# Reciprocal of the softmax sums before the transpose instead of behind it, and another place for the routing constants, in a fused attention and mixture kernel

## The chip, the cores and the metric

One Trainium2 chip, one of its cores. The metric is the device time of one execution in microseconds (us). The engines are named as in the profile: PE (matrix products; PEld is its weight loading), DVE (vector), ACT (scalar), POOL (GpSimd) and SP (here only issues transfers).

## The reference, cut to what matters

Attention over 4 batches of 8 heads, 576 positions of 64 elements, causal and with a decay bias; its output goes through a three-way max layer and then through a routed layer with one of 8 experts for each of the 2304 tokens.

```python
def _attn_ref(q, k, v, s):
    scores = scale * np.matmul(q, k.transpose(0, 1, 3, 2))
    ...
    bias = -(cum[:, :, :, None] - cum[:, :, None, :])
    scores = np.where(causal, -1000000000.0, scores + np.minimum(bias, 0.0))
    attn = np.exp(scores - np.max(scores, axis=-1, keepdims=True))
    attn = attn / (np.sum(attn, axis=-1, keepdims=True) + 1e-09)
    return np.matmul(attn, v)

def _moe_ref(x, w1, w2, w3, w_out):
    h = np.maximum(np.maximum(x @ w1, x @ w2), x @ w3)
    return h @ w_out

def _moe2_ref(x, modality_id, w_gate, modality_bias, w1, w2):
    logits = x @ w_gate + modality_bias[modality_id]
    e_idx = np.argmax(logits, axis=1)
    ...
    for e in range(E):
        h = np.maximum(x[e_idx == e] @ w1[e], 0.0)
        out[e_idx == e] = gate_w[e_idx == e, None] * (h @ w2[e])
```

The change touches the division by the sums (with the 1e-09 added to them) and the time at which constants of the routing are prepared: the table of token numbers, the bias of the modality, an upper triangle for counting.

## The kernel before, in words

The work has three stages: attention (up to about 250 us), the three-way max layer with its output product and the routing (to about 550 us), and the experts (to the end). Products in near float32 precision are made of three passes over a rounded high part and a low part, which ACT rounds and DVE or POOL subtracts.

Attention goes through 16 couples of heads (`for p in range(1, NP)` with couple 0 ahead of it); a couple shares the 128 partitions for its values. For each head `front` loads the head that is three ahead (L_AHEAD), splits the next one (`split`, S_AHEAD) and calls `scores`. There the 576 rows fall into five chunks of 128 rows (QC), and six banks of scores are made: two matmuls each into a tile `s_ps` of a pool of three banks (lines 248 and 249), one DVE reduction that scales, masks and takes the row minimum `mn` (line 250), and an exponential on ACT for each chunk that also sums into `l` (line 252). The scaled scores stand in one of four buffers `e`. Every couple has one tile `l` of 128 rows by 2 heads x 5 chunks.

A couple's remaining work is put off: `turn()`, which calls `inverse` for couple p - 1, runs after the first head of couple p, and `drain` then turns the two heads (`turned`: 15 transposes a head through four tiles `t_ps` of a pool of three banks, each copied into a `pt` by ACT or DVE in turn) and multiplies them with the values (`values_of`: twelve matmuls in a fixed order, then two DVE multiplications with `rb`, lines 301 and 302). `inverse` transposes `l` to 10 rows of 128 (line 261) into a tile of that same pool `t_ps`, adds 1e-9 on ACT on the way out of it (line 263), takes the reciprocal on DVE (line 264), stores the result to DRAM and loads it back spread over 64 partitions for each head as `rb` (lines 265 and 268).

When the four couples of a batch are done, first-layer products for it (`fill`, lines 149 to 153, with the `h` maxima of line 325) are put between the heads that follow, by a list `todo` of due times. Weights are converted early in couples 1 to 8 (`convert`, `converted`).

`tables()` (lines 372 to 401) prepares the constants: seven transfers on SP, five instructions on POOL and seven on DVE, none on ACT or PE. It is called in couple 12 (`P_SET`), inside `tc.issue_after(exps[-1])`.

A scheduler sets the order on every engine: it goes through the program with estimated times and places what is ready; `tc.issue_after(x)` keeps the marked instructions behind `x` where both are on one engine. So the order in the program is not the order on the engines, and each engine then executes its own in order and waits for the others by semaphores.

Of the kernel before, what the change touches and what calls it, by code (L numbers as in the profile page):

```python
# [5 lines left out]
F32 = mybir.dt.float32  # L6
# [3 lines left out]
ALU = mybir.AluOpType  # L10
ACTF = mybir.ActivationFunctionType
# [75 lines left out]
def fused_kernel(tc, qk, vd, sd, w64, mod, wg, wgt, mb, we, cst, csi, out):  # L87
    nc = tc.nc
    V, A, G, P, SP = nc.vector, nc.scalar, nc.gpsimd, nc.tensor, nc.sync
    top = ExitStack()  # L90
    with top:
# [13 lines left out]
        ident = per.tile([128, 128], F32, name="ident")  # L105
# [5 lines left out]
        bias = per.tile([128, NT, E], F32, name="bias")  # L111
# [45 lines left out]
        with ExitStack() as es:  # L157
# [17 lines left out]
            ss = es.enter_context(tc.tile_pool(name="ss", bufs=4))  # L175
# [5 lines left out]
            mask = ap1.tile([128, S], F32, name="mask")  # L181
# [11 lines left out]
            last_load = [None]  # L193


            def load(p, j):
                x = qkp.tile([128, 2, S], F32, name="qk_r", bufs=QR_BUFS)
                k_b = qkp.tile([66, S], F32R, name="k_b", bufs=KB_BUFS)
                for t in (range(2) if p == 0 else ()):
                    (SP, A)[t if j == 0 else 0].dma_start(out=x[:, 1 - t], in_=qk[PORD[p], :, 1 - t, j])  # L200
                if p == 0:
                    A.dma_start(out=k_b.bitcast(F32)[64:66], in_=augk.bitcast(F32)[16 * j + PORD[0]:16 * j + PORD[0] + 1])
                    if j == 0:
                        SP.dma_start(out=mask[:, S - 128:S], in_=cst[:, 256:384])
                        SP.dma_start(out=ident, in_=cst[:, 0:128])
                else:
                    SP.dma_start(out=x, in_=qk[PORD[p], :, :, j])
                    last_load[0] = SP.dma_start(out=k_b.bitcast(F32)[64:66], in_=dk[PORD[p], :, j]).ins
                return p, j, x, k_b


            def split(t):
                p, j, x, k_b = t
                hl = qkp.tile([128, 2, S], F32R, name="hl", bufs=HL_BUFS)
                q_b = qbs[(2 * p + j) % len(qbs)]
                A.copy(out=hl[64:128, 0], in_=x[64:128, 1])
                A.copy(out=hl[:, 1], in_=x[:, 0])
                G.tensor_copy(out=k_b[0:64], in_=x[0:64, 1])
                V.tensor_tensor(out=hl[0:64, 0], in0=x[64:128, 1], in1=hl.bitcast(F32)[64:128, 0], op=ALU.subtract)  # L219
                ins = G.tensor_tensor(out=q_b[0:64], in0=x[0:64, 0], in1=hl.bitcast(F32)[0:64, 1], op=ALU.subtract).ins  # L220
                return ins, (hl, q_b, k_b)

            def values_in(p):
                v_r = vp.tile([128, 5, 128], F32, name="v_r")
                SP.dma_start(out=v_r, in_=vd[PORD[p]])
                return v_r

            def scores(j, qkb):
                hl, q_b, k_b = qkb
                e = e_bufs[n_e[0] % E_N]  # L230
                n_e[0] += 1
                mn = ss.tile([128, 5], F32, name="mn")
                if j == 0:
                    sums.append(ss.tile([128, 2, 5], F32, name="l"))
                l = sums[-1][:, j]
                banks = [None] * len(SPACK)
                for c, (q0, _, w) in enumerate(QC):

                    nq = 128
                    ec = e[:, EOFF[c]:EOFF[c] + w]  # L240
                    m0 = 448 if c == 0 else S - w
                    first = 3.0e38
                    for k0, n in [(0, w)] if c < 4 else [(0, 288), (288, 288)]:
                        bi, o = next((i, o) for i, bank in enumerate(SPACK) for cc, kk, o in bank if (cc, kk) == (c, k0))
                        if banks[bi] is None:
                            banks[bi] = ps_s.tile([128, 512], F32, name="s_ps")
                        s_ps = banks[bi][0:nq, o:o + n]
                        P.matmul(s_ps, hl[:, 1, q0:q0 + nq], hl[:, 0, k0:k0 + n], start=True, stop=False)  # L248
                        ins = P.matmul(s_ps, q_b[:, q0:q0 + nq], k_b[:, k0:k0 + n], start=False, stop=True).ins  # L249
                        V.tensor_tensor_reduce(out=ec[:, k0:k0 + n], in0=s_ps, in1=mask[0:nq, m0 + k0:m0 + k0 + n], scale=-0.125, scalar=first, op0=ALU.add, op1=ALU.min, accum_out=mn[0:nq, c:c + 1])  # L250
                        first = mn[0:nq, c:c + 1]
                    ex = A.activation(out=ec, in_=ec, func=ACTF.Exp, bias=mn[0:nq, c:c + 1], scale=-1.0, accum_out=l[0:nq, c:c + 1]).ins  # L252
                    if c >= 2:
                        gates.append(ins)
                exps.append(ex)
                return e


            def inverse(p, l):
                r_ps = ps_t.tile([128, 512], F32, name="t_ps")[0:10, 0:128]  # L260
                P.transpose(out=r_ps, in_=l.rearrange("p j c -> p (j c)"), identity=ident)
                r_t = ss.tile([10, 128], F32, name="r_t")
                A.activation(out=r_t, in_=r_ps, func=ACTF.Copy, bias=1e-9)
                V.reciprocal(out=r_t, in_=r_t)
                SP.dma_start(out=r_d[p], in_=r_t)
                rb = vp.tile([128, 640], F32, name="rb")
                for j in range(2):
                    SP.dma_start(out=rb[j * 64:(j + 1) * 64], in_=r_d[p:p + 1, 5 * j:5 * j + 5].rearrange("a c n -> a (c n)").to_broadcast([64, 640]))
                return rb
# [59 lines left out]
            parts = {0: load(0, 0)}  # L329
# [10 lines left out]
            def front(h):  # L340
                n = h + L_AHEAD
                if n < 2 * NP:
                    parts[n] = load(*divmod(n, 2))
                n = h + S_AHEAD
                if n < 2 * NP:
                    parts[n] = split(parts[n])[1]
                return scores(h % 2, parts.pop(h))

            behind = []
# [1 line left out]
            exps = []  # L351
            sums = []
            last_t = [None]

            def drain(keep):
                while len(behind) > keep:
                    p, es_, v_r, rbs, pts = behind.pop(0)
                    pts.append(turned(es_[len(pts)], len(pts)))
                    if len(pts) == 2:
                        values_of(p, v_r, rbs[0], pts)  # L360
# [45 lines left out]
            for p in range(1, NP):  # L406
                v_r = values_in(p)
                es_ = []
                for j in range(2):
                    es_.append(front(2 * p + j))  # L410
                    if j == 0:
                        turn()
                    drain(1 - j)
                    if j == 1:
                        turn = queue(p, es_, v_r)
                    n_head += 1
                    while todo and todo[0][0] < n_head:
                        at, job = todo.pop(0)
                        with tc.issue_after(gates[int(at * 3)]):
                            job()  # L420
                if p == NP - 1:
                    turn()
                    drain(0)
                with tc.issue_after(exps[-1 - CONV_LAG]), tc.issue_after(last_load[0]):
                    for w in raws:
                        converted(*w)
                    raws = [convert(n // 3, n % 3, w0p, "w0", rawp, early=True) for n in CONV.get(p, ())]
                if p == P_SET:
                    with tc.issue_after(exps[-1]):
                        tables()  # L430
                if p % (H // 2) == H // 2 - 1:
                    b = PORD[p] // (H // 2)
                    n = 0
                    for i in range(b * S // FW, (b + 1) * S // FW if NFILL[b] else 0):
                        xx, hs = [], {}
                        todo.append((n_head + FILL_0 + n * FILL_N[b] / (6 * NFILL[b]), lambda i=i, xx=xx: xx.extend(fill_x(i, fxp, "fx", V if XL_V else G))))
                        for f in range(NFILL[b]):
                            for j in range(3):
                                todo.append((n_head + FILL_0 + n * FILL_N[b] / (6 * NFILL[b]), lambda i=i, f=f, j=j, xx=xx, hs=hs: fill(i, f, j, xx, hs, ps_f, fhp, "fh")))
                                n += 1  # L440
# [467 lines left out]
```

## Time and profile before

| what | value |
|---|---|
| median of 3 runs | 752.18 us (748.55 to 752.93) |
| the profiled execution | 752.2 us |
| its span, first to last instruction | 750.3 us |
| PE busy | 719.6 us (96%) |
| DVE busy | 529.4 us (71%) |
| ACT busy | 404.4 us (54%) |
| POOL busy | 181.6 us (24%) |

The busy times are of the whole span, and the stages differ: an engine with a low share can still set the pace of one of them. A matmul's end is modelled, so a PE that counts as busy need not go at its full rate. Idle time of an engine is put down to the event that ended it.

### The profile page before, as it was taken

To read this page: it belongs to the slowest core of one execution; us is meant where nothing else is said; L and a number is where in the kernel's file an instruction comes from. 1 tells how busy PE (TensorE), PEld (TensorE's weight loads), DVE (VectorE), ACT (ScalarE), POOL (GpSimd) and SP (SyncE) were. 2 spreads that over 40 slices of the span, in tenths; PEclk is the share of its full clock that TensorE was granted. 3 is DMA by queue.
4 is the path that set the end of the run, shared out by engine and by line. 5 is a ranking of instruction groups with operands and counts; after the bars stand their busy time and mean duration, and the time that the engine had idled before them with its cause. 6 is when DMAs were issued, how large, how long until landed. Compare 5 with 4: busy or idle time off the path is not lost. (4 is left out here: it accounts for less than half of the span.)

```text
span 750.3 us, 13624 instructions
## 1 busy us (share of the span) xinstructions
PE 719.6 (96%) x4602; PEld 642.7 (86%) x4602; DVE 529.4 (71%) x1567; ACT 404.4 (54%) x976; POOL 181.6 (24%) x202
## 2 busy tenths in 40 slices
PE   3898999899999999999999999999999999999996
PEld 3665798788998899899999898989899988999884
DVE  6899979987776589692958796737677556575540
ACT  6887878876775445222222322536546556565631
POOL 6346554544340100010010101032222222222101
PEclk9999999999999999999999999999899999999999
DMA  8476665674321174101101101847547675756610
GB/s 234 132 233 206 211 200 171 192 240 141 113 71 46 41 271 153 37 14 22 43 22 53 50 21 51 282 146 219 182 156 234 213 252 181 244 212 208 230 40 18
DMA packets 45104, 108.56 MB, mean 145 GB/s; under 512 B 8992, under 2 KB 12992, under 8 KB 45024
## 3 DMA queue, kind: packets, MB, share of 16 engines
q1 hardware_dynamic: 37368, 90.75, 37.3%
q0 software_dynamic: 4912, 11.82, 5.0%
q10 hardware_dynamic: 2744, 5.02, 1.9%
q8 instruction: 38, 0.62, 0.4%
q14 instruction: 42, 0.34, 0.1%
HBM read 93.55 MB, written 12.18 MB: 141 GB/s over the span
## 5 line engine op out<-in xcount | busy, mean ns | idle before, releaser
L149 PE MATMUL a_ps<-xh,w_h 128*128 128x384 f32 (+2 forms) x492 | 159.0, 324 | 0.2
L152 PE MATMUL a_ps<-xl,w_h 128*128 128x384 f32 (+2 forms) x492 | 158.2, 322 | 0.0
L153 PE MATMUL a_ps<-xh,w_l 128*128 128x384 f32 (+2 forms) x492 | 157.1, 320 | 0.0
L608 DVE TENSOR_TENSOR e_l<-e_raw,e_h 128x512 fp32r<-128x512 f32 x160 | 103.3, 687 | 15.6 <-ACT e_h L607 9.8
L607 ACT CAST e_h<-e_raw 128x512 fp32r<-128x512 f32 x160 | 93.1, 623 | 21.5 <-DMA e_raw<-in_we 7.6
L252 ACT ACTIVATE e<-e,mn 128x64 f32<-128x64 f32 (+4 forms) x160 | 89.2, 559 | 17.7 <-DVE mn L250 17.4
L149 PEld LDWEIGHTS a_ps<-xh,w_h 128*128 128x128 f32 x492 | 92.6, 188 | 1.6 <-DVE h L325 0.6
L152 PEld LDWEIGHTS a_ps<-xl,w_h 128*128 128x128 f32 x492 | 92.6, 188 | 0.4
L153 PEld LDWEIGHTS a_ps<-xh,w_l 128*128 128x128 f32 x492 | 92.6, 188 | 0.2
L248 PE MATMUL s_ps<-hl 128*128 128x64 f32 (+2 forms) x192 | 66.3, 356 | 16.4 <-DVE hl L219 9.2
L641 PE MATMUL h_ps<-x2t,e_h 128*128 128x256 f32 x288 | 81.8, 285 | 0.0
L642 PE MATMUL h_ps<-x2t,e_l 128*128 128x256 f32 x288 | 81.5, 284 | 0.0
L638 PE MATMUL h_ps<-x2t,e_h 128*128 128x256 f32 x288 | 80.9, 286 | 0.0
L495 DVE CUSTOM_DVE_ANT_0 junk<-x,wg 128x512 bf16<-128x512 f32 x96 | 66.0, 688 | 16.9 <-ACT x L569 16.0
L519 POOL DMA_INDIRECT table<-meta,si x18 | 19.5, 1081 | 230.9 <-DVE mx L499 96.6
L277 PE MATMUL t_ps<-ident,e 128*128 128x128 f32 x480 | 71.4, 280 | 2.2 <-DVE pt L280 1.6
L250 DVE CUSTOM_DVE_ANT_0 e<-s_ps,mask 128x64 f32<-128x64 f32 (+4 forms) x160 | 63.2, 421 | 4.6 <-PE s_ps L249 3.7
L277 PEld LDWEIGHTS t_ps<-ident,e 128*128 128x128 f32 x480 | 56.8, 143 | 6.6 <-DVE pt L280 3.5
L669 PE MATMUL y_ps<-e_h,gh 128*128 128x512 f32 x152 | 61.3, 403 | 0.4 <-ACT gh L661 0.4
L249 PE MATMUL s_ps<-k_b,q_b 66*128 66x64 f32 (+2 forms) x192 | 60.1, 322 | 0.9 <-DMA k_b<-augk 0.9
L671 PE MATMUL y_ps<-e_h,gl 128*128 128x512 f32 x152 | 60.7, 399 | 0.0
L670 PE MATMUL y_ps<-e_l,gh 128*128 128x512 f32 x152 | 59.8, 394 | 0.0
(176 smaller groups left out, 1485.3 us busy)
## 6 DMA issues: line engine op xcount, KB each, us to landing
e_raw<-in_we SPq DMA_DIRECT2D x80, 512.0 KB
qk_r<-in_qk SPq DMA_DIRECT2D x30, 576.0 KB
w_raw<-in_w SPq DMA_DIRECT2D x24, 512.0 KB
v_r<-in_vd SPq DMA_DIRECT2D x16, 320.0 KB
rb<-r_d SPq DMA_DIRECT2D x32, 160.0 KB
x2d<-x ACTq DMA_DIRECT2D x18, 256.0 KB
w_h<-w_z POOLq DMA_DIRECT2D x9, 256.0 KB, 3.9
wg<-in_wg SPq DMA_DIRECT2D x4, 512.0 KB
```

What stands on the lines that cost most here:

```text
L149: ins = P.matmul(a_ps, wh[:, c], xh[:, c], start=c == 0, stop=False).ins
L152: P.matmul(a_ps, wh[:, c], xl[:, c], start=False, stop=False)
L153: P.matmul(a_ps, wl[:, c], xh[:, c], start=False, stop=c == 3)
L248: P.matmul(s_ps, hl[:, 1, q0:q0 + nq], hl[:, 0, k0:k0 + n], start=True, stop=False)
L252: ex = A.activation(out=ec, in_=ec, func=ACTF.Exp, bias=mn[0:nq, c:c + 1], scale=-1.0, accum_out=l[0:nq, c:c + 1]).ins
L277: last_t[0] = P.transpose(out=t_ps[:, n * 128:(n + 1) * 128], in_=e[:, EOFF[c] + kb * 128:EOFF[c] + (kb + 1) * 128], identity=ident).ins
L495: V.tensor_tensor_reduce(out=junk, in0=x2, in1=wg_sb[ei // 2][:, ei % 2, :], scale=1.0, scalar=0.0, op0=ALU.mult, op1=ALU.add, accum_out=l ...
L607: A.copy(out=h, in_=raw[:, a])
L608: V.tensor_tensor(out=lo, in0=raw[:, a], in1=h.bitcast(F32), op=ALU.subtract)
L638: ins = P.matmul(h_ps, w(hs, f, c), xt[:, 0, c], start=c == 0, stop=False).ins
L641: P.matmul(h_ps, w(hs, f, c), xt[:, 1, c], start=False, stop=False)
L642: P.matmul(h_ps, w(ls, f, c), xt[:, 0, c], start=False, stop=c == 3)
```

## The change

`inverse` now adds 1e-9 to `l` on ACT (128 partitions of 10) and takes the reciprocal there on DVE, before the transpose; the transposed values are copied out by ACT as they are. The call of `tables()` now stands behind three marks, the last DVE reduction of the scores, the last subtraction of `split` on POOL and the last load of `k_b` on SP, instead of behind the last exponential on ACT.

```diff
-                        V.tensor_tensor_reduce(out=ec[:, k0:k0 + n], in0=s_ps, ..., op1=ALU.min, accum_out=mn[0:nq, c:c + 1])
+                        last_v[0] = V.tensor_tensor_reduce(out=ec[:, k0:k0 + n], in0=s_ps, ..., op1=ALU.min, accum_out=mn[0:nq, c:c + 1]).ins
...
             def inverse(p, l):
+                r = ss.tile([128, 10], F32, name="r")
+                A.activation(out=r, in_=l.rearrange("p j c -> p (j c)"), func=ACTF.Copy, bias=1e-9)
+                V.reciprocal(out=r, in_=r)
                 r_ps = ps_t.tile([128, 512], F32, name="t_ps")[0:10, 0:128]
-                P.transpose(out=r_ps, in_=l.rearrange("p j c -> p (j c)"), identity=ident)
+                P.transpose(out=r_ps, in_=r, identity=ident)
                 r_t = ss.tile([10, 128], F32, name="r_t")
-                A.activation(out=r_t, in_=r_ps, func=ACTF.Copy, bias=1e-9)
-                V.reciprocal(out=r_t, in_=r_t)
+                A.copy(out=r_t, in_=r_ps)
                 SP.dma_start(out=r_d[p], in_=r_t)
...
-                    parts[n] = split(parts[n])[1]
+                    last_g[0], parts[n] = split(parts[n])
...
                 if p == P_SET:
-                    with tc.issue_after(exps[-1]):
+                    with tc.issue_after(last_v[0]), tc.issue_after(last_g[0]), tc.issue_after(last_load[0]):
                         tables()
```

The scheduler makes another order of it on every engine. On DVE, at the start, between the last reduction of head 0 (`e_132`) and those of head 1 (`e_133`), before:

```order
L387 COPY meta<-tok 128x18
L250 ISA e_133,mn<-s_ps,mask 128x64
L250 ISA mn 128x1
L250 ISA e_133,mn<-s_ps,mask 128x192
L250 ISA mn 128x1
L219 TENSOR_TENSOR hl<-qk_r,hl 64x576
L250 ISA e_133,mn<-s_ps,mask 128x320
L250 ISA mn 128x1
L391 TENSOR_SCALAR mod_b<-mod_i 128x18
L250 ISA e_133,mn<-s_ps,mask 128x448
L250 ISA mn 128x1
L393 CAST m_2810<-mod_b 128x18
```

And at the same place now (an "ISA" row with `e` is a reduction of line 250, the row behind it reads out its minimum):

```order
L250 ISA e_133,mn<-s_ps,mask 128x64
L250 ISA mn 128x1
L250 ISA e_133,mn<-s_ps,mask 128x192
L250 ISA mn 128x1
L219 TENSOR_TENSOR hl<-qk_r,hl 64x576
L250 ISA e_133,mn<-s_ps,mask 128x320
L250 ISA mn 128x1
L250 ISA e_133,mn<-s_ps,mask 128x448
L250 ISA mn 128x1
L250 ISA e_133,mn<-s_ps,mask 128x288
L250 ISA mn 128x1
```

The instructions of `tables()` are gone from between the reductions of heads 1 and 2. On DVE they now stand in the scores of head 26 (`e_134` there; the rows of the changed kernel have its own line numbers, up to 4 higher):

```order
L250 ISA e_134,mn<-s_ps,mask 128x320
L250 ISA mn 128x1
L391 COPY meta<-tok 128x18
L250 ISA e_134,mn<-s_ps,mask 128x448
L250 ISA mn 128x1
L250 ISA e_134,mn<-s_ps,mask 128x288
L250 ISA mn 128x1
L395 TENSOR_SCALAR mod_b<-mod_i 128x18
L397 CAST m_2834<-mod_b 128x18
L399 TENSOR_SCALAR m_2836<-m_2834 128x18
L403 TENSOR_TENSOR bias<-m_2834,mb_sb 128x144
L404 TENSOR_TENSOR bias_2840<-m_2836,mb_sb 128x144
```

Their transfers stand on SP, all seven in a row, between the load of `k_b` for head 28 and the load of `qk_r` for head 31. On PE, the first transposes, of couple 0 (`l` its sums, `e_132` its first head), stood right behind the six score banks of head 2 and ahead of those of head 3, before:

```order
L248 MATMUL s_ps<-hl 128x288
L249 MATMUL s_ps<-k_b,q_b_131 128x288
L261 MATMUL t_ps<-ident,l 10x128
L277 MATMUL t_ps<-ident,e_132 128x128 x8
L248 MATMUL s_ps<-hl 128x64
L249 MATMUL s_ps<-k_b,q_b_129 128x64
L248 MATMUL s_ps<-hl 128x192
L249 MATMUL s_ps<-k_b,q_b_129 128x192
L248 MATMUL s_ps<-hl 128x320
L249 MATMUL s_ps<-k_b,q_b_129 128x320
L277 MATMUL t_ps<-ident,e_132 128x128 x7
```

Now they stand behind four banks of head 3 (`q_b_129`), and the rest of head 0's transposes behind the first bank of head 4 (`q_b_130`):

```order
L248 MATMUL s_ps<-hl 128x448
L249 MATMUL s_ps<-k_b,q_b_129 128x448
L264 MATMUL t_ps<-ident,r 10x128
L279 MATMUL t_ps<-ident,e_132 128x128 x8
L248 MATMUL s_ps<-hl 128x288
L249 MATMUL s_ps<-k_b,q_b_129 128x288
L248 MATMUL s_ps<-hl 128x288
L249 MATMUL s_ps<-k_b,q_b_129 128x288
L248 MATMUL s_ps<-hl 128x64
L249 MATMUL s_ps<-k_b,q_b_130 128x64
L279 MATMUL t_ps<-ident,e_132 128x128 x7
```

The transposes of the couples after it move in the same way, most by about a head.

## Rows read from the trace of the kernel before

**Rows 1.** The page's busy times, part 1.
```profile
span 750.3 us, 13624 instructions
...
PE 719.6 (96%) x4602; PEld 642.7 (86%) x4602; DVE 529.4 (71%) x1567; ACT 404.4 (54%) x976; POOL 181.6 (24%) x202
```

**Rows 2.** Busy time by stretch: length, PE, PEld, DVE, ACT, POOL, clock, DMA.
```profile
13.67:20.00 6.33, 5.69 (x18) 4.78 (x18) 5.55 (x24) 5.61 (x18) 4.42 (x6) 1.00 0.83 225
20.00:80.00 60.00, 52.72 (x337) 39.35 (x338) 54.59 (x158) 47.91 (x133) 29.24 (x28) 0.97 0.60 186
80.00:160.00 80.00, 77.38 (x596) 66.95 (x595) 72.31 (x214) 65.62 (x183) 42.66 (x42) 1.00 0.64 201
160.00:260.00 100.00, 99.84 (x784) 87.75 (x784) 67.89 (x212) 64.93 (x182) 28.08 (x28) 1.00 0.32 96
```

**Rows 3.** Waits of PE, 0 to 80 us: total us, times, longest.
```profile
PE s_ps L248 <- DVE hl L219: 9.2, 1, 9.2
PE s_ps L248 <- DVE mn L250: 4.6, 6, 1.7
...
PE s_ps L248 <- DMA qk_r<-in_qk: 0.5, 1, 0.5
```

**Rows 4.** Waits of DVE, 20 to 160 us.
```profile
DVE x L301 <- PE o_ps L300: 6.3, 4, 2.8
```

**Rows 5.** DVE in order of time, 15 to 25 us: start, duration, instruction.
```profile
16.71 0.17 DVE L387 COPY meta<-tok 128x18 int32<-128x18 int32 x1
...
18.66 0.87 DVE L391 TENSOR_SCALAR mod_b<-mod_i 128x18 int32<-128x18 int32 x1
...
19.99 0.47 DVE L393 CAST m<-mod_b 128x18 f32<-128x18 int32 x1
...
22.13 0.30 DVE L401 TENSOR_TENSOR bias<-bias,bias 128x144 f32<-128x144 f32 x1
```

**Rows 6.** Groups by line: count, busy us, mean ns, idle before.
```profile
L264 DVE RECIPROCAL r_t<-r_t 10x128 f32<-10x128 f32 x16 | 14.9, 934 | 0.2 <-ACT r_t L263 0.2
...
L263 ACT ACTIVATE r_t<-t_ps 10x128 f32<-10x128 f32 x16 | 4.2, 260 | 7.0 <-PE t_ps L261 7.0
...
L512 DVE RECIPROCAL meta<-sm 128x1 f32<-128x1 f32 x18 | 2.9, 161 | 0.0
```

**Rows 7.** Line 264 alone by stretch: length, DVE busy and count, clock, DMA.
```profile
20.00:80.00 60.00, 3.73 (x4) 0.97 0.60 186
80.00:160.00 80.00, 5.61 (x6) 1.00 0.64 201
```

**Rows 8.** Order of time, 32 to 42 us, and one group by line.
```profile
32.73 0.66 PE L277 MATMUL t_ps<-ident,e 128*128 128x128 f32 x4
...
33.97 0.67 ACT L252 ACTIVATE e<-e,mn 128x448 f32<-128x448 f32 x1
...
34.54 0.19 ACT L252 ACTIVATION_READ_ACCUMULATOR e<-e,mn 128x1 f32 x1
...
39.99 0.52 DVE L250 CUSTOM_DVE_ANT_0 e<-s_ps,mask,mn 128x288 f32<-128x288 f32 x1
...
41.42 0.61 DVE L280 COPY pt<-t_ps 128x448 f32<-128x448 f32 x1
...
L282 ACT COPY pt<-t_ps 128x448 f32<-128x448 f32 x64 | 31.5, 495 | 10.3 <-PE t_ps L277 8.4 <-PE s_ps L248 1.8
```

**Rows 9.** SP in order of time, 28 to 34 us.
```profile
29.87 0.27 SPq L265 DMA_DIRECT2D r_d<-r_t  x1
...
32.68 1.14 SPq L268 DMA_DIRECT2D rb<-r_d  x2
```

**Rows 10.** Busy time by stretch, as rows 2; the clock is the third last.
```profile
60.00:65.00 5.00, 4.12 (x16) 1.53 (x18) 4.54 (x8) 3.96 (x10) 2.70 (x4) 0.66 0.89 259
505.00:510.00 5.00, 5.00 (x23) 4.39 (x23) 4.26 (x20) 3.28 (x9) 2.29 (x3) 0.68 0.32 108
540.00:546.00 6.00, 5.79 (x31) 5.57 (x30) 2.39 (x18) 1.47 (x4) 3.95 (x4) 0.52 0.34 100
```

More of the change, by code (lines that the diff above doesn't have):

```diff
@@ L249, in scores @@
                         ins = P.matmul(s_ps, q_b[:, q0:q0 + nq], k_b[:, k0:k0 + n], start=False, stop=True).ins
-                        V.tensor_tensor_reduce(out=ec[:, k0:k0 + n], in0=s_ps, in1=mask[0:nq, m0 + k0:m0 + k0 + n], scale=-0.125, scalar=first, op0=ALU.add, op1=ALU.min, accum_out=mn[0:nq, c:c + 1])
+                        last_v[0] = V.tensor_tensor_reduce(out=ec[:, k0:k0 + n], in0=s_ps, in1=mask[0:nq, m0 + k0:m0 + k0 + n], scale=-0.125, scalar=first, op0=ALU.add, op1=ALU.min, accum_out=mn[0:nq, c:c + 1]).ins
                         first = mn[0:nq, c:c + 1]
@@ L353, in fused_kernel @@
             last_t = [None]
+            last_v = [None]
+            last_g = [None]
             def drain(keep):
```

## The prediction

> **What bounds the kernel now.** I read the totals first [rows 1]: the program spans 750.3 us and the PE is busy for 719.6 us of them, so only some 31 us of the span can be won without taking work off the PE, and this change takes none off it. I then cut the span into stretches [rows 2]. The reader is to see three things in them. From 160 us to the end of attention the PE is busy all the time (99.84 of 100 us), so nothing that the other engines save there can shorten the kernel. Between 13.67 and 160 us the PE is idle for 0.64, 7.28 and 2.62 us, 10.5 us together. And in the stretch from 20 to 80 us the PE issues 337 matmuls in 60 us, 5.6 per us, against 7.5 per us from 80 to 160 and 7.8 from 160 to 260: its busy time there holds waiting too. The engine that is full in that stretch is DVE: 54.59 of 60 us, with ACT at 47.91.
>
> The waits of the PE say the same [rows 3]. Its first 9.2 us are the lead-in, up to the first `hl`, which the change leaves alone. After that its largest wait up to 80 us is for `mn`, DVE's scaled and masked scores (4.6 us in 6 waits): the three banks of `s_ps` are full and DVE has not emptied one. DVE itself sits idle for about 5.4 of the 60 us, and the longest of its waits is for the value matmuls, which come in one block on the PE: the multiplication of `x` waited for `o_ps` 6.3 us in four waits, one of them 2.8 us [rows 4]. So up to about 80 us, which is before the first-layer products of the finished batch have begun to fill the PE, the kernel goes at the pace of DVE; from 80 to 160 us DVE and the PE are both nearly full; after that the PE alone counts.
>
> **The change part by part.** *The table constants.* `tables()` is called behind the 13th couple, but its mark was an ACT instruction and it issues none on ACT, so its seven DVE instructions stand at the very start, between the scores of heads 1 and 2. They took 0.87, 0.47, twice 0.17 and three times 0.30 us [rows 5] (one of each is shown), 2.6 us together, between 16.7 and 22.4 us, where DVE is the engine waited for. Gone from there, I count 0.9 of it (DVE's share busy, 54.59 of 60): 2.3 us won. The seven SP transfers go too, but the PE's only wait for a load of `qk_r` up to 80 us is 0.5 us [rows 3], so I cost that at nothing; should one be late by its own issue, it is earlier now, never later.
>
> The seven come back inside the scores of head 26, past 200 us. DVE then holds 2.6 us more work in a stretch where it is busy 67.89 of 100 us and the PE is the bound [rows 2]. It also waits in order for `tok`, which SP issues as the fifth of the new transfers behind the `h_d` store. SP issued the load that depends on a small store 2.8 us after the store, and one issue took it 0.27 to 0.57 us [rows 9], so the six issues ahead of `tok` take some 2.5 us and `tok` lands some 5.3 us after that store's `h`; between `h` and `meta` DVE has ten instructions of its own, at about 0.5 us each as those of rows 8, so the wait is between 0 and 1 us. Behind it on DVE stand the scores' reductions and the `h` maxima, which the PE needs. I take 0.5 us lost for the whole move; bounds 0 (all covered by the PE) and 3.5 (all of it on the path).
>
> [...]
>
> *The reciprocals.* Sixteen of 10x128 take 934 ns each; the only other reciprocal, of one element a partition, takes 161 ns [rows 6]. Between them lie 127 elements, so one element costs (934-161)/127 = 6.1 ns and ten cost 161 + 9 x 6.1 = 216 ns, an estimate from these two rows; bounds 161 and 300. Each saves 0.72 us of DVE. Four of them lie between 20 and 80 us, six between 80 and 160 and the other six later [rows 7]. The four are worth 4 x 0.72 = 2.9 us where DVE sets the pace. The six could give 4.3 us, but there the PE was idle for only 2.62 us, and the value blocks made part of that; I take 1.0 us. The last six are worth nothing: the PE was busy throughout.
>
> [...]
>
> *The addition on ACT.* Sixteen new ACT instructions of 128x10. The nearest row is the ACT copy with the same bias, 260 ns [rows 6]; that copy stays, without the bias, at the same cost. ACT is at 47.91 of 60 us in the DVE stretch, and four additions make 1.0 us there. The PE waits for ACT rarely; I take 0.3 us lost, bounds 0 and 1.0.
>
> *What moves.* The transpose of the sums stands ahead of the couple's other transposes, because its tile is the first that they take from the pool `t_ps`. Until now it needed only the sums; now it needs an ACT addition and a DVE reciprocal, and both engines put these behind the scores of the next heads. So in the first couple the transposes start after four banks of head 3 rather than after head 2, most of a head later. There are four `e` buffers, so the scores of head 4 need the transposes of head 0, which now end right in front of them. The tightest loop I see: the exponential of 448 columns (0.67 + 0.19 us), ACT's copy of `pt` (0.50), four transposes (0.66) [rows 8] and the first scores of head 4, which I put at 0.4 us: 2.4 us, during which DVE has one copy of 0.61 us and two reductions of up to 0.52 [rows 8], 1.7 us. That leaves about 0.7 us of DVE idle a couple, 2.8 us over the four couples up to 80 us. On the other side the block of value matmuls comes later, behind more banks of scores, so that DVE has work while it runs; that can give back the 2.8 us of the longest wait [rows 4]. Bounds: 2.8 lost and 2.8 won; I take 0.9 lost, nearer the loss, since the loop is in every couple and the wait of 2.8 us was there once.
>
> *The sum.* Won: 2.3 + 2.9 + 1.0 = 6.2 us. Lost: 0.5 + 0.3 + 0.9 = 1.7. Net 4.5 us less. The profiled execution took 752.2 us for its span of 750.3 (1.9 us lie around it), and the median of the three runs is 752.18, so the two agree: 752.2 - 4.5 = 747.7 us. The first matmul, the stages behind attention and the last transfers stay as they are.
>
> **The rivals.** *The stretch empties wholly.* DVE's relief and the better place of the value blocks remove all PE idleness after the lead-in: 10.5 us, 741.7. For it speaks the low rate of matmuls from 20 to 80 us, which shows more to win than the idle rows. [...] Against it: the transposes have less slack than before.
>
> *The relief is not passed on.* DVE finishes sooner and waits for the PE or ACT instead, because in-order blocks and four `e` buffers set the pace; or the move costs what it saves. Time 752 give or take 1.5. For it: DVE already had 5.4 us of idle time in the stretch where I call it the bound.
>
> *Slower: the transposes a head late starve DVE in every couple.* Place: the reductions of head h + 4 against the transposes of head h. If each of the ten couples up to 160 us pays the mean of DVE's waits for `o_ps`, 6.3/4 = 1.6 us [rows 4], that is 15.8 us lost against 6.2 won: 761.8. It is slower than before from 0.62 us a couple on, if the fills do not cover it. Against it: beyond 80 us fill matmuls stand between the transposes and keep the PE busy, so six of the ten couples can hardly pay in full.
>
> **How the numbers follow.** The forecast, 745 to 750.5, gets 0.48, the full gain 0.20, no gain 0.18 and the slower case 0.14. The later falls of the PE clock (0.68 from 505 to 510 us and 0.52 from 540 to 546 us, [rows 10]) cost 1.6 and 2.9 us and lie in stages that the change does not touch; if one comes or goes, the time moves by that much either way, and the runs before already span 4.4 us. The range of 740.5 to 758 takes in the full gain with such a margin, and nearly half the slower case. About 1%, 7.5 us, is what can be told from no change here, that is under 744.7 or over 759.7. Faster: nine tenths of the full gain and a fifth of the forecast, 0.18 + 0.09 = 0.27. Slower: the slower case and a hundredth of the rest, 0.15. Within 1%: 0.58.
>
> **What would show it.** Right: the reciprocals at 0.19 to 0.25 us and the additions at 0.2 to 0.3; no table instruction on DVE before 190 us; the stretch from 20 to 80 us with more than 337 matmuls, some 5 us of work more; the PE full by 155 us rather than 160; the stages after it the same and only earlier. Wrong: DVE's busy share from 20 to 80 us well under 0.85 with the PE's idle time unchanged (relief not passed on); waits of `t_ps` for `pt`, or of DVE's reductions for transposes, of over 0.62 us a couple (the slower case); PE idle time near 205 us, where SP and DVE now handle the tables.

## The result, and the profile after

The changed kernel takes 758.15 us (median of 4 runs, 755.19 to 760.16) against 750.37 us for the kernel before on the same chip (4 runs, 748.47 to 752.93): a ratio of 1.0101, 95% interval 1.0069 to 1.0133. It is slower by about 1%, 7.8 us; the forecast was 4.5 us less. The profiled execution took 756.76 us.

The page's totals of the changed kernel, to be read against [rows 1]:

```profile
span 754.9 us, 13625 instructions
...
PE 718.9 (95%) x4602; PEld 643.6 (85%) x4602; DVE 525.3 (70%) x1567; ACT 405.6 (54%) x992; POOL 179.8 (24%) x202
```

DVE has 4.1 us less to do and the span is 4.6 us longer: work was saved and time was lost. The operations cost what was forecast or less. The changed kernel's line 262 (the reciprocal) and line 261 (the addition), each with its count and the least, median and longest ns, and its first and last start in us:

```profile
L262 DVE RECIPROCAL r<-r x16: 204/210/218, 24.2 to 251.5; 128x10 f32<-128x10 f32 x16
...
L261 ACT ACTIVATE r<-l x16: 194/206/221, 23.9 to 251.3; 128x10 f32<-128x10 f32 x16
```

So the reciprocal went from 934 ns [rows 6] to 210, forecast 216; the addition takes 206, forecast 260. The constants come late, with the wait forecast as 0 to 1 us at 1.39 (SP's issue, then DVE; in brackets the idle time ahead):

```profile
200.89 0.43 SPq L390 DMA_DIRECT2D tok<-in_csi  x1
...
203.33 0.18 DVE L391 COPY meta<-tok 128x18 int32<-128x18 int32 x1 [1.39 <-DMA tok<-in_csi]
```

The stretches, with the columns of [rows 2], the last row one that was not shown of before:

```profile
20.00:80.00 60.00, 51.42 (x340) 39.97 (x340) 52.02 (x160) 50.22 (x145) 29.15 (x30) 0.97 0.68 209
80.00:160.00 80.00, 74.44 (x567) 63.43 (x566) 68.78 (x195) 59.93 (x170) 40.26 (x41) 1.00 0.58 182
160.00:260.00 100.00, 98.15 (x774) 87.52 (x773) 67.29 (x221) 66.08 (x192) 29.83 (x35) 1.00 0.33 99
...
110.00:125.00 15.00, 11.56 (x87) 10.49 (x87) 14.01 (x43) 13.87 (x39) 10.29 (x11) 1.00 0.43 134
```

PE is idle for 1.30 us more from 20 to 80 us, 2.94 more from 80 to 160 (74.44 for 77.38 busy) and 1.69 more from 160 to 260, where it had been full. DVE's busy time from 20 to 80 us fell by 2.57 us, so its relief is there, and PE's idle time grew all the same. The largest hole is at 110 to 125 us: PE 11.56 us busy of 15, and in the kernel before

```profile
110.00:125.00 15.00, 14.69 (x117) 12.92 (x116) 14.06 (x40) 11.72 (x33) 5.79 (x7) 1.00 0.61 187
```

with DVE as busy as before (14.01 and 14.06 us). What differs is the order of DVE's work in it. DVE of the changed kernel, in order of time, ahead of the longest hole, and PE's first matmul behind it, which waited 2.62 us for a reduction:

```profile
118.09 0.69 DVE L130 SCALAR_TENSOR_TENSOR w_z<-w_raw,w_z 128x512 int32<-128x512 int32 x1
118.69 0.42 DVE L282 COPY pt<-t_ps 128x256 f32<-128x256 f32 x1
119.14 1.52 DVE L219 TENSOR_TENSOR hl<-qk_r,hl 64x576 fp32r<-64x576 f32 x1
120.69 0.69 DVE L131 SCALAR_TENSOR_TENSOR w_z<-w_raw,w_z 128x512 int32<-128x512 int32 x1
121.30 0.48 DVE L250 CUSTOM_DVE_ANT_0 e<-s_ps,mask 128x320 f32<-128x320 f32 x1
...
121.85 0.40 PE L248 MATMUL s_ps<-hl 128*128 128x288 f32 x1 [2.62 <-DVE mn L250]
```

From 118.09 to 121.30 us, 3.2 us, DVE does a weight's conversion (lines 130 and 131), a copy of `pt` and the low part of a coming head (line 219) one after the other, and no reduction, while PE waits for a free bank of scores. The same lines in the kernel before, in order of time:

```profile
117.19 0.68 DVE L130 SCALAR_TENSOR_TENSOR w_z<-w_raw,w_z 128x512 int32<-128x512 int32 x1
117.79 0.42 DVE L280 COPY pt<-t_ps 128x256 f32<-128x256 f32 x1
118.12 0.62 DVE L250 CUSTOM_DVE_ANT_0 e<-s_ps,mask 128x448 f32<-128x448 f32 x1
...
119.04 0.79 DVE L131 SCALAR_TENSOR_TENSOR w_z<-w_raw,w_z 128x512 int32<-128x512 int32 x1
119.75 0.50 DVE L250 CUSTOM_DVE_ANT_0 e<-s_ps,mask,mn 128x288 f32<-128x288 f32 x1
...
120.44 2.31 DVE L219 TENSOR_TENSOR hl<-qk_r,hl 64x576 fp32r<-64x576 f32 x1
```

There the subtraction of line 219 even took 2.31 us rather than 1.52, but reductions stand between the others and right ahead of it, and PE goes on. How far attention is shows best in the 16 multiplications of a couple's values (line 301 before, 303 after: first and last start). Before:

```profile
L301 DVE TENSOR_TENSOR x<-o_ps,rb x16: 677/692/693, 38.1 to 261.4; 128x512 f32<-128x512 f32 x16
```

After:

```profile
L303 DVE TENSOR_TENSOR x<-o_ps,rb x16: 628/691/694, 40.7 to 267.2; 128x512 f32<-128x512 f32 x16
```

The last comes 5.8 us later. From 13.67 us to there PE's idle time is 10.7 us before and 16.1 after, so 5.4 of the 5.8 us are PE that waits (before, then after):

```profile
13.67:261.36 247.69, 236.99 (x1744) 200.10 (x1745) 201.70 (x606) 184.55 (x515) 104.41 (x103) 0.99 0.50 155
```

```profile
13.67:267.17 253.50, 237.40 (x1752) 202.07 (x1753) 197.82 (x605) 185.95 (x530) 103.40 (x107) 0.99 0.50 151
```

The sixth couple's multiplication is still 0.9 us ahead; two couples later the changed kernel's is 8.4 us behind (before, then after):

```profile
108.70 0.69 DVE L301 TENSOR_TENSOR x<-o_ps,rb 128x512 f32<-128x512 f32 x1 [1.92 <-PE o_ps L300]
136.89 0.69 DVE L301 TENSOR_TENSOR x<-o_ps,rb 128x512 f32<-128x512 f32 x1 [1.30 <-PE o_ps L300]
```

```profile
107.82 0.69 DVE L303 TENSOR_TENSOR x<-o_ps,rb 128x512 f32<-128x512 f32 x1 [1.80 <-PE o_ps L302]
145.24 0.68 DVE L303 TENSOR_TENSOR x<-o_ps,rb 128x512 f32<-128x512 f32 x1
```

The busy times between these two multiplications, before and after:

```profile
108.70:136.89 28.19, 27.88 (x222) 24.42 (x219) 25.40 (x75) 22.50 (x62) 12.92 (x15) 1.00 0.63 189
```

```profile
107.82:145.24 37.42, 33.98 (x267) 30.21 (x264) 32.71 (x86) 29.33 (x83) 21.70 (x21) 1.00 0.54 172
```

Most of the 9.2 us between them (from 0.9 ahead to 8.4 behind) are not lost: the new order puts 45 matmuls more into this stretch (first-layer products and scores) that stood elsewhere before. Lost is PE's idle time, 3.4 us for 0.3: 3.1 of the 5.4 us. None of the constants' instructions stands there.

### The profile page after: what moved, and what is told of

It is laid out like the page before. It is cut to its first block, busy times and chain, and to the rows that moved or that the text cites. A ratio compares the mean times of both kernels' runs of the same rounds, so it can differ in the third digit from the quotient of the medians.

```text
span 754.9 us, 13625 instructions
## 1 busy us (share of the span) xinstructions
PE 718.9 (95%) x4602; PEld 643.6 (85%) x4602; DVE 525.3 (70%) x1567; ACT 405.6 (54%) x992; POOL 179.8 (24%) x202
## 3 DMA queue, kind: packets, MB, share of 16 engines
q1 hardware_dynamic: 37368, 90.75, 38.1%
## 5 line engine op out<-in xcount | busy, mean ns | idle before, releaser
L252 ACT ACTIVATE e<-e,mn 128x576 f32<-128x576 f32 (+4 forms) x160 | 88.8, 556 | 25.8 <-DVE mn L250 25.5
L248 PEld LDWEIGHTS s_ps<-hl 128*128 128x128 f32 x192 | 39.5, 207 | 24.1 <-DVE mn L250 12.6
```

## The experiments

**One part alone.** Theory A: the transposes come late because they wait for the reciprocal. Theory B: the late constants cost.

```diff
 e1_recip_only: inverse() as changed; tables() behind exps[-1] as before
 e2_tables_only: inverse() as before; tables() behind the three marks
```

> Only the reciprocal moved ahead of the transpose; the constants stay at the start. Theory A (the transposes that wait for the sums come about a head late and DVE and PE then wait for each other): slower than before by the whole amount or more, 755 to 762 us, with PE idle from 80 to 160 us at 5 us or more (before 2.6). Theory B (the constants in head 26 and what they displace cost the time): 744 to 749, PE idle from 160 to 260 us as before (0.2). Theory C (any new order of the attention engines costs some us, whatever part makes it): 752 to 758, with the idle time at other places than in the changed kernel.

> Only the constants moved; the reciprocal stays behind the transpose. Theory A: no slower than before, 746 to 751, the first transposes right behind head 2 as before. Theory B: slower, 753 to 758, with PE idle of about 2 us or more between 195 and 260 us. Theory C: 752 to 758, idle time at places that neither of the two kernels has.

The reciprocal alone took 751.38 us, ratio 1.0032 [1.0011, 1.0052]; the constants alone 762.08, 1.0153 [1.0103, 1.0202]. Neither time lies in a range that a theory had given. And the parts don't add up: the constants alone cost at least as much as both together. In e2 the large holes of PE stand ahead of 90 us, far from where the constants now are; between 195 and 260 us, where theory B looked for 2 us or more, PE is idle for 0.05 us. Busy time of e2 by stretch:

```profile
60.00:65.00 5.00, 2.41 (x13) 1.72 (x13) 4.97 (x12) 2.75 (x7) 1.68 (x3) 0.89 0.46 136
65.00:70.00 5.00, 4.76 (x14) 2.65 (x16) 4.47 (x15) 3.69 (x13) 1.42 (x2) 0.50 0.69 191
```

PE was busy for 2.41 of 5 us, and in the next 5 its granted clock was 0.50, where it had been 0.89.

**The sums' transpose out of the way.** In the changed kernel and in the kernel before, the transpose takes its tile from the bank of the value products, so that the other transposes no longer wait behind it.

```diff
-                r_ps = ps_t.tile([128, 512], F32, name="t_ps")[0:10, 0:128]
+                r_ps = ps_o.tile([128, 512], F32, name="o_ps")[0:10, 0:128]
```

> The changed kernel, but the transpose of the sums writes the bank of the value products instead of one of the three banks that the couple's transposes take in turn, so these no longer stand behind the reciprocal. Theory A: the time falls below before, 742 to 749, since the relief of DVE stays and the delay goes. Theory B: 752 to 757, the loss past 200 us stays. Theory C: anywhere in 748 to 760.

> The kernel before, with the same other bank for the transpose of the sums. It is the control for the run above: theory A says 746 to 752 (the sums' transpose was not late before, little to win) and the changed kernel with this bank 3 us or more under it, theory B says 746 to 752 and the changed kernel with this bank above it, theory C gives no sign.

With it the changed kernel took 752.71 us, 1.0035 [1.001, 1.0059]: some 5 us faster, as theory A had the sign, but not below the kernel before, as it had the size. And the kernel before, which has no longer chain to hide, became slower by the same edit: 758.79, 1.0109 [1.0068, 1.015], which neither theory A nor B had. Each of these edits makes a new order, and the order before beats all of them.

**The constants late, the order kept.** The kernel before, unchanged at the start, prepares a second set of the constants, which nothing reads, behind the three marks.

```diff
-                        tables()
+                        scratch = tables()
+                    with tc.issue_after(last_v[0]), tc.issue_after(last_g[0]), tc.issue_after(last_load[0]):
+                        tables_2(scratch)
```

> The kernel before with its constants at the start as they are, and a second set of them, written to tiles that nothing reads, behind the 13th couple as in the changed kernel. The order of PE is that of before up to head 23. Theory B (the late constants cost the time): 753 to 760, with PE idle between 195 and 260 us. Theory D (the late place is nearly free, and the time is lost earlier, where the constants' leaving lets the scheduler make another order): 748 to 752.

749.4 us, 1.0012 [0.9982, 1.0043]: the late place costs nothing that can be measured. Theory B falls. What is left for e2 is that the constants' leaving the start makes another order; e9 and e12 below put that to the test.

**The low part of K on POOL.** Theory D: in the new orders DVE's subtraction of line 219 meets POOL's more often and is slowed.

```diff
-                V.tensor_tensor(out=hl[0:64, 0], in0=x[64:128, 1], ...)
+                G.tensor_tensor(out=hl[0:64, 0], in0=x[64:128, 1], ...)
```

> The changed kernel with the subtraction that makes the low part of K (line 219) on POOL instead of DVE. Theory D, in its sharper form: in every order seen so far that subtraction, when it begins while POOL is in a run of its own, lasts until POOL is done (3.81 us instead of 0.75 in the run with the constants alone moved), and DVE, PE and the clock pay for it. Without it on DVE the three kernels with their different orders come together: 738 to 748 here, within 3 us of the next two. If the orders themselves cost the time and the collisions do not, the three stay 5 us or more apart, in the order before, changed, constants only.

> The kernel before with line 219 on POOL. Theory D: 740 to 748, and the changed kernel with the same edit equal or up to 4 us faster. Orders alone: 742 to 752, the changed kernel 5 us or more slower. A third case: POOL becomes late with the low part, which the scores need, and both are slower than 752.

> Only the constants moved, with line 219 on POOL. Theory D: the 12.8 us that the constants alone cost fall to 3 or less against the kernel before with the same edit, 740 to 750. Orders alone: 755 or more.

799.47 us, 1.0634 [1.0588, 1.0681] (changed kernel); 788.65, 1.0484 [1.0419, 1.0549] (before); 770.44, 1.0256 [1.0199, 1.0312] (constants alone). On POOL the subtraction takes 1.41 us instead of 0.75, each kernel has yet another order, and the three are up to 29 us apart, with the constants alone, which had been the slowest, now the fastest. This settles nothing on theory D.

**The order itself.** Now the order is taken as a part of its own. A table in the kernel holds, engine by engine, the order in which attention's instructions stand in one kernel, and the operations of another are put in it by order-only marks (issue order, no wait). The instructions that the change itself adds or moves stay free.

```diff
+        for e, mine in chain.items():
+            for a, b in zip(ORDER[e], ORDER[e][1:]):
+                tc.add_manual_dep(mine[b], mine[a].name, ... NoSync ...)
```

> The late constants of e2, but every engine's attention instructions are held in the order of before (the instructions of the constants alone find their own place, behind their three marks). Theory E (the slower time is the order that the scheduler makes): 1.015 goes; what is left is the 2.3 us of DVE work taken off the start, 0.996 to 1.000, about 746.5 to 749.5 us, and PE idles less than 10.7 us between 13.67 and 260 us. Rival F (the constants cost where they stand now, or POOL, SP or DVE are hurt by their new place, whatever the order): it stays at about 1.015.

> The early reciprocal of e1, every engine's other attention instructions held in the order of before (the addition on ACT and the reciprocal on DVE find their own place between them). Theory E: DVE's relief of 0.72 us a couple is now passed on, 0.993 to 0.999, about 744 to 748.5 us. Rival F (the longer chain sums, ACT, DVE, transpose costs by itself): 1.003 as e1, or above, since PE's transposes stand earlier than the chain can serve.

> The changed kernel's operations, all of them, in the order of before. Theory E: below before by what e9 and e10 win together, 0.990 to 0.998, about 742 to 748 us; PE idle between 13.67 and 260 us under 10 us. Rival F: 1.010 as the changed kernel, about 757.

> The mirror: the operations of before (reciprocal on 10 partitions behind the transpose, constants at the start) in the changed kernel's order. Theory E: as slow as the changed kernel or slower, since DVE also has the long reciprocals and the early constants: 1.010 to 1.02, about 757 to 765 us. Rival F: 1.000, about 749.

| operations | order | us | ratio to before |
|---|---|---|---|
| constants late (e9) | before's | 747.05 | 0.998 [0.9957, 1.0004] |
| early reciprocal (e10) | before's | 750.77 | 1.0024 [0.9997, 1.0052] |
| both (e11) | before's | 748.02 | 0.9996 [0.9968, 1.0024] |
| those of before (e12) | the changed kernel's | 761.07 | 1.0179 [1.0122, 1.0236] |

This is the clean cut. The changed kernel's operations in the old order are level with before; the old operations in the new order are as slow as the changed kernel or slower. No run held a kernel's own operations in its own order; that e9 and e11 are level with before says that the holding by itself costs little. Theory E's numbers hold for e9 and e12; e11 lies just above its range (0.990 to 0.998), with PE idle for 12.7 us where it said under 10, and for e10 it said 0.993 to 0.999, a miss: the order's price is confirmed, a gain of the reciprocal is not. The values' multiplications of e9, then of e12:

```profile
L310 DVE TENSOR_TENSOR x<-o_ps,rb x16: 676/692/693, 34.9 to 256.8; 128x512 f32<-128x512 f32 x16
```

```profile
L310 DVE TENSOR_TENSOR x<-o_ps,rb x16: 679/691/693, 45.9 to 274.5; 128x512 f32<-128x512 f32 x16
```

In e9 the first couple is 3.2 us earlier than before (34.9 for 38.1) and the last 4.6. How far two such traces differ by themselves shows e5, whose order is that of before up to head 23:

```profile
L301 DVE TENSOR_TENSOR x<-o_ps,rb x16: 675/691/692, 37.1 to 259.4; 128x512 f32<-128x512 f32 x16
```

It is 1.0 us ahead of before at the first couple and 2.0 at the last; the trace of before is that of a run above its median. Against e5, e9 is 2.2 and 2.6 us earlier. In e12 the last couple is 13.1 us later than before, far outside that. Its order puts more scores ahead of the first couple, which is 7.8 us later (in the changed kernel 2.6). And between the sixth and the eighth couple e12 does what the changed kernel does, with the old operations:

```profile
113.98:151.96 37.98, 34.50 (x267) 30.22 (x264) 33.55 (x86) 29.20 (x81) 20.82 (x21) 1.00 0.54 171
```

```profile
126.62 0.76 DVE L228 TENSOR_TENSOR hl<-qk_r,hl 64x576 fp32r<-64x576 f32 x1
...
128.56 0.41 PE L257 MATMUL s_ps<-hl 128*128 128x288 f32 x1 [2.57 <-DVE mn L259]
```

The same 267 matmuls, 3.5 us idle for 3.4, and the same hole of PE, 2.57 us for 2.62: at this place it is the order that loses the time. The low part of K (line 228 here) takes 0.76 us in e12 and 1.52 in the changed kernel, so theory D's slowed subtraction does not by itself make this hole (in e12 the conversion ahead of it is the slower one, 1.22 us for 0.69; the series lasts 3.0 us for 3.2). The waits of PE up to 160 us (line 257 of e12 is the scores, 259 the reductions, 286 the transposes) say the same; the kernel before:

```profile
PE s_ps L248 <- DVE mn L250: 6.4, 9, 1.7
...
PE t_ps L277 <- DVE pt L280: 1.6, 3, 0.7
```

And e12:

```profile
PE s_ps L257 <- DVE mn L259: 12.4, 15, 2.6
...
PE t_ps L286 <- DVE pt L289: 2.2, 3, 1.3
```

The changed kernel's own are 9.6 and 4.1 us.

e10 adds one of another kind (line 273 is the transpose of the sums, 271 the reciprocal):

```profile
PE t_ps L273 <- DVE r L271: 3.9, 3, 1.6
```

In the old order the transpose stands too early for the longer chain, and PE waits 3.9 us for it.

**Was the relief on DVE worth anything?** Theory G: yes, and that wait takes it back. Theory H: it was never on the path. In e13 and e15 the sums' transpose has its own bank, as in e3, and all of `inverse` is free within the old order; in e14 the reciprocal is left out, so that the values are not divided by their sums. The tokens then go to other experts, and of its time only attention can be read.

```diff
 e13: e11 with r_ps from ps_o, inverse() not held
 e14: before in its own order, without
-                V.reciprocal(out=r_t, in_=r_t)
 e15: e10 with r_ps from ps_o, inverse() not held
```

> Both parts in the order of before, but the transpose of the sums goes into the bank of the value products and, with what hangs on it, is free to stand where its reciprocal is ready. Theory G (relief is real, the wait for the reciprocal takes it back): below e9 by the relief, 0.991 to 0.996, about 742 to 746 us, with the wait of PE for the reciprocal under 0.5 us in all and PE idle under 8 us between 13.67 and 260 us. Theory H (relief was never on the path): as e9, 0.997 to 1.000.

> The reciprocal is left out (16 times 0.93 us of DVE gone, the chain no longer than before); everything else is before, in the order of before, constants at the start. Theory G: 0.993 to 0.997, about 744 to 747 us: the 2.9 us of the four early ones and some of the next six. Theory H: 0.999 to 1.001.

> e13 with the constants at the start as before: the early reciprocal alone, its transpose in the other bank and free. Theory G: 0.994 to 0.998, under e10 by 3 to 5 us. Theory H: 1.000 to 1.002, as e10 or e10 less its 3.9 us of wait only where DVE is not the next bound.

e15 took 749.79 us, 1.0012 [0.9996, 1.0027]; e13 746.28, 0.9948 [0.9928, 0.9967]; e14 898.63, 1.1988 [1.1959, 1.2017], which is the experts' stage. Its attention, by the values' multiplications:

```profile
L309 DVE TENSOR_TENSOR x<-o_ps,rb x16: 680/691/692, 38.4 to 260.8; 128x512 f32<-128x512 f32 x16
```

Without any reciprocal the last one starts at 260.8 us, in the kernel before at 261.4 and in e5 at 259.4. Sixteen times 0.93 us of DVE, 14.9 us, are worth 0.6 us, which is less than the 2 us by which before and e5 differ: nothing that can be told. DVE's waits of e14, 20 to 160 us, say where it goes:

```profile
DVE x L309 <- PE o_ps L308: 6.7, 5, 2.8
DVE pt L288 <- PE t_ps L285: 4.8, 8, 1.3
DVE h L333 <- PE a_ps L162: 1.8, 2, 1.3
```

And before, the transposes alone:

```profile
DVE pt L280 <- PE t_ps L277: 1.6, 4, 0.5
```

The wait for `o_ps` is much the one of before (6.3 us, [rows 4]); DVE now waits 4.8 us for the transposes instead of 1.6, and 1.8 us for first-layer products instead of 0.4. That is theory H: a DVE that is done sooner waits for PE. e15 fits it too: without e10's 3.9 us of wait, the early reciprocal is level with before and not better. e13 is the one version whose interval lies wholly below both kernels. Its ratio is in theory G's range, but PE is idle for 11.0 us from 13.67 to 260 us where theory G said under 8, and its first and last multiplication are no earlier than e9's (the traced execution took 748.53 us and was the slowest of its six):

```profile
L312 DVE TENSOR_TENSOR x<-o_ps,rb x16: 628/692/693, 35.1 to 259.5; 128x512 f32<-128x512 f32 x16
```

Its interval overlaps that of e9, so what it wins can be the constants' part alone; whether the early reciprocal adds to it there is not settled.

## Why the prediction was wrong

**The step that failed** is "What moves". I took the new order as 0.9 us lost, with bounds of 2.8 either way, worked out from one loop at the first couples. Between the changed operations in the old order (e11, 0.9996) and the same operations in the new one (the changed kernel, 1.0101) lies the order's price: 1.05%, 7.9 us; with the old operations it is 1.8%, 13 us (e12). I had named the kind of wait right, PE against DVE's reductions, but had looked at the first couple and at one loop. More than half of PE's added idle time (3.1 of 5.4 us) came where I had not looked, in two couples with weight conversions and first-layer products between the heads. From the forecast (4.5 us won) to the result (7.8 lost) there are 12.3 us: 7.0 of them are this term (7.9 lost for 0.9), and 3.9 the next.

**The reciprocals, 2.9 + 1.0 us won**, failed too: removed altogether they give 0.6 us (e14), no more than two traces differ. The size of the saving was right (0.72 us each); what was wrong was to count the first four in full because DVE was busy for 91% of their stretch. A busy share does not say that the others wait for this work: PE and DVE wait for each other by turns (PE 4.6 us for `mn` up to 80 us, [rows 3]; DVE 6.3 us for `o_ps` from 20 to 160 us, [rows 4]). The rival "the relief is not passed on" was right here, at 0.18.

**The constants leaving the start, 2.3 us won**, was right in its mechanism: with the order kept, attention's last couple comes 4.6 us sooner than in the trace of before and 2.6 sooner than in e5's (e9), and the medians differ by 1.6 us, 0.2%, an interval that just includes no gain. **The late constants, 0.5 lost**: the second set late costs 1.0012, nothing measured (e5); the wait for `tok` was 1.4 us where 1 was the most, though from its issue to the copy only 2.4 us passed (203.33 - 200.89), less than the 2.8 that I took. **The addition on ACT, 0.3 lost**: 206 ns each, below the 260 taken; but as a link of the chain it costs PE up to 3.9 us of wait where the transpose is not moved (e10). That was priced within "What moves".

**The slower rival** (761.8 us) had the right sign and nearly the right time, not the right mechanism. It let each couple pay for transposes that come a head later. They do not come that late: counted by the banks of scores ahead of them on PE, the first nine couples' transposes moved by 0.1 to 1.0 head, 0.5 on average, and of the last seven only one moved (the account of the change had said "most by about a head"). And the lateness is not what costs. In e2 the transposes stand within 0.5 head of their old place, and it loses 1.5%; in e1 they stand about as late as in the changed kernel, and it loses 0.3%. The forecast's own signs went both ways. For it were the reciprocals at 210 ns, the additions at 206 and no table instruction ahead of 190 us; against it the stretch from 20 to 80 us with 340 matmuls for 337, where some 5 us of work more were forecast, and PE not full by 155 us.

What stays open: which of the moved instructions the order's loss hangs on. The stretch at 119 us, the same in e12, is one place of several, and no run moved single instructions.

## What to carry to other kernels

Where a scheduler makes the order from estimated times, an edit is two changes: its operations and a new order, and the second can be the larger (here 8 to 13 us lost, against 1 to 3 won or lost). Separate them before judging either: hold the old order and put in the new operations, then the old operations in the new order. And price a saving on a nearly full engine by leaving the work out in the same order, not by its busy share.

## What the runs showed of the hardware

DVE's subtraction of line 219 (64x576) takes 753 to 755 ns mostly, and up to 3812 in e2:

```profile
L219 DVE TENSOR_TENSOR hl<-qk_r,hl x32: 753/755/3812, 7.9 to 228.1; 64x576 fp32r<-64x576 f32 x32
```

It ran from 57.69 for 3.81 us, to 61.50. POOL at the same time, in order of time:

```profile
57.49 1.41 POOL L220 TENSOR_TENSOR q_b<-qk_r,hl 64x576 fp32r<-64x576 f32 x1 [1.05 <-ACT hl L217]
58.87 0.78 POOL L314 TENSOR_TENSOR xl<-x,xh 128x288 fp32r<-128x288 f32 x1
59.62 1.25 POOL L136 TENSOR_TENSOR w_l<-w_z,w_h 128x512 fp32r<-128x512 f32 x1
```

POOL had begun a subtraction 0.2 us earlier and did two more without a pause, to 60.87; DVE's ended 0.63 us after that, a little less than it takes alone. So here it looks as if it had waited for POOL's whole run. The two longer ones shown above, 1.52 and 2.31 us, also ran beside POOL's `q_b` subtraction (changed kernel, then before):

```profile
118.15 1.89 POOL L220 TENSOR_TENSOR q_b<-qk_r,hl 64x576 fp32r<-64x576 f32 x1 [1.86 <-ACT hl L217]
```

```profile
120.70 1.42 POOL L220 TENSOR_TENSOR q_b<-qk_r,hl 64x576 fp32r<-64x576 f32 x1
```

Both of DVE's ended 0.62 to 0.63 us after POOL's (120.66 for 120.04, 122.75 for 122.12). The traces show what runs beside a long subtraction, not what holds it. Over all fourteen traces that have this subtraction on DVE, 130 of its 448 took more than 0.9 us (before 8 of 32, the longest 2.31), and each of these ended 0.60 to 0.64 us after some instruction of POOL did. That need not be the end of POOL's run: in 59 of the 130 POOL had gone straight on with its next. Behind the one at 57.69 us PE was busy for only 2.41 us of the 5 from 60 us, and the granted clock was 0.50 in the next 5. An order of one engine thus also decides which instructions of two engines meet. What these meetings cost in time is not shown: beyond 0.755 us each, they lengthen the subtractions by 6.2 us in all before, 8.5 in the changed kernel, 9.0 in e12, 12.7 in e1 and 14.4 in e2, and e1, which has twice as much as before, is only 0.3% slower.
